# Two blocks of 512 tokens taken together, one inner tile of 1024 tokens at a time

## The chip, the cores and the metric

The kernel runs on one core of a Trainium2 chip. The metric is device time in microseconds, the median over timed runs. Before the change it is 786.54 us (two runs, 785.62 and 787.46). One further execution was taken by the hardware profiler; all durations below come from that one.

The engines of the core are TensorE (PE in the rows: matmuls, with the weight loads shown apart as PEld), VectorE (DVE), ScalarE (ACT), GpSimd (POOL, here mostly the issuer of DMAs) and SyncE (SP, an issuer of DMAs). Each runs its own instructions in program order and waits on semaphores for the others.

## The reference

`x` has 8 batches of 3008 tokens by 256 channels, `filt_r` and `filt_i` 1505 x 256. All in float32:

```python
X = np.fft.rfft(x, axis=1)
y = np.fft.irfft(X * (filt_r + 1j * filt_i)[None], n=3008, axis=1)
h = y.reshape(24064, 256) @ w_in            # w_in 256 x 2048
g = np.maximum(h, 0) + alpha * np.minimum(h, 0)
out = g @ w_out                             # w_out 2048 x 256
```

So there is a filter along the sequence by Fourier transforms, and then a two-layer network with a leaky activation whose slope `alpha` differs from one inner unit to the next.

## The kernel before

**The transforms.** 3008 is 47 x 64, and the transforms are matmuls with constant matrices in float16. Per batch there are 16 pieces A (`piece_a`, one matmul of 512 columns), 12 pieces B (`piece_b`, two matmuls of 256 columns; then two DVE multiplications with the filter, `ww` and `uu`, L232 and L233, which read PSUM; then two accumulating DMAs from POOL that join the complex parts, L235), 12 pieces C (`piece_c`, two matmuls of 256) and 16 pieces D (`piece_d`, four matmuls of 94 columns). Between A and B and between C and D the data goes through DRAM to be turned. D leaves `yT`, the input of the network with channels on partitions; it holds two batches. Pieces A, C and D are copied out of PSUM by ACT. They share two PSUM banks (`psF`), whose order is the string `BANKS`.

**The network.** The tokens are taken in 48 blocks: 512 tokens, and 384 in one of every twelve so that two batches make twelve blocks. A block has 16 steps. In step `j`, `up` multiplies 128 inner units by the block: two matmuls of 512 columns (L497) into one half of a PSUM tile `hps` of two banks; there are two such tiles. After every odd step ACT copies the two inner tiles, 128 x 1024, to float16 in `gtb` (L505). DVE then forms `m = min(g, 0) * (alpha - 1)`, in two instructions of 512 because the two inner tiles have different slopes (L508, slopes in `alm_s`), and adds it, `g += m`, in one instruction of 1024 (L509). In what follows one such copy with its DVE instructions is called a **unit**; a block of 512 tokens has eight. `gtb` holds two blocks; `m` has two buffers.

**The second layer** of a block runs one block later, woven into the steps of the next (`LAG` 16 steps; the loop sends its matmuls until `done` reaches `(step - 16) / 16` blocks). A plain block sends 64 matmuls of 256 columns (`eight`, L534). A block in `FAST` uses seven products of half size in place of eight (`seven`, L556): 112 matmuls of 128 columns, on the quarters `a11, a21, a12, a22` of `g` and on combinations of them and of the weights. The combinations of the weights are computed once (`combine`, into `tw_s`). Those of `g` are four sums, each in two halves `h`: `z1 = a21 + a22` and `z2 = z1 + a11` on DVE (L517, L519), `a21 += a11` and `a12 += z2` by accumulating DMAs from POOL (L521, L523). At the end of a fast block ACT copies partial products out (five copies of 256) and DVE joins them by a subtraction and an addition in float32 (L476). 21 of the 48 blocks are fast, up to block 38 every second one.

**The order** is written out by hand: 48 x 16 = 768 steps, and tables (`STEPS_A` to `STEPS_X`, `FIRST` for the first batches, `SUMS` and `TAIL` for the sums) that say before which step a piece goes. In a step come, in this order, the joining operations left over (`flush`), the sums that are due, the pieces that are due, the two `up` matmuls, and the second layer's matmuls up to `done`. Batch 0 is transformed before step 0 by a method of its own (`First`) while the constants arrive.

Of the kernel before, what the change touches and what calls it, by code (L numbers as in the profile page):

```python
# [13 lines left out]
NFFT = 3008  # L14
# [8 lines left out]
    "010101010101010101010101010101001010010110010010101010101010101010110101101010101010101011010101"  # L23
    "010101010101010101010110110101001011010101011010110111010010101010101010010110100010101110101101"
    "010010101100101010010101010101010101001101010101010010110111010110101010101010101010101010101001"
    "010101010100101101101010010101010101010101010101010101100101101010110100100010100101010101010101"
    "01010101010101101010101101001110101010101010101010101010"
)
STEPS_A = (-84, -81, -77, -76, -65, -59, -58, -58, -56, -53, -52, -51, -50, -48, -46, -43)
STEPS_B = (-21, -15, 4, 6, 13, 21, 25, 27, 32, 40, 54, 55)  # L30
STEPS_C = (2, 10, 16, 19, 24, 33, 35, 46, 62, 63, 70, 70)
STEPS_D = (89, 89, 90, 91, 92, 94, 95, 98, 100, 101, 105, 113, 118, 125, 144, 147)
STEPS_T = (0, 0, 2, 2, 13, 17, 19, 21, 21, 35, 40, 43)
STEPS_E = (6, 6, 7, 11, 23, 27, 29, 29, 53, 54, 55, 56)
STEPS_N = (24, 29, 35, 37)
STEPS_K = (118, 121, 128, 133, 143)
STEPS_X = ((20, 27, 42, 52), (107, 109, 113, 126))
FIRST = (
# [61 lines left out]
def kernel(  # L100
# [90 lines left out]
    def obank():  # L191
        ob[0] ^= 1
        return psO[ob[0]].tile([128, 2, D], FP32, name="op")

    class Fft:
        def __init__(self, b):
            self.b = b
# [529 lines left out]
```

## Time and profile before

| | |
|---|---|
| median of the timed runs | 786.54 us |
| profiled execution, its own time | 781.17 us |
| its span, first to last instruction | 779.1 us |
| granted TensorE clock | 1.000 |
| ACT busy, 902 instructions | 605.1 us (78%) |
| POOL busy, 361 instructions | 273.4 us (35%) |
| DMA moved | 122.93 MB, mean 158 GB/s |

Busy time is the union of an engine's instruction times. Instructions of one engine overlap in the rows: a duration is from start to the end of the last write, while the next may start earlier. What an engine needs is therefore counted by pitches, the distance from one start to the next in a stretch without idle time. "x" counts instructions. A release after an arrow names what ended the idle time before an instruction.

### The profile page before, as it was taken

What the parts mean: (1) busy time and instruction counts of PE and PEld (TensorE: products, weight loads), DVE (VectorE), ACT (ScalarE), POOL (GpSimd) and SP (SyncE); (2) the same over time, 40 slices, a digit from 0 to 9 for tenths busy, and PEclk for the clock granted to TensorE, in tenths of its full rate; (3) what the DMA queues carried; (4) which work ended last, traced back from release to release, by engine and by line L of the source; (5) the groups of instructions that cost most, each with busy time, mean ns of one, the idle gap of its engine ahead of it and who ended that gap; (6) DMA issues with size and microseconds to landing.
All of it is one profiled execution on the core that took longest, in us unless ns stands there. A gap on an engine that the chain in (4) does not pass through costs nothing.

```text
span 779.1 us, 18298 instructions
## 1 busy us (share of the span) xinstructions
PE 759.0 (97%) x6952; PEld 540.7 (69%) x6952; DVE 687.3 (88%) x1501; ACT 605.1 (78%) x902; POOL 273.4 (35%) x361
## 2 busy tenths in 40 slices
PE   7898999999999999999999999999999999999998
PEld 6755667666677767766667767767667777777766
DVE  4786996799999999899899989989899999889994
ACT  4687778888878887788868887788878777787763
POOL 7720542144244341453324423434223434102210
PEclk9999999999999999999999999999999999999999
DMA  9994868766997779975799769886797555735642
GB/s 192 187 224 121 163 121 189 207 123 146 198 211 169 147 152 199 214 164 122 163 215 190 147 136 196 197 169 130 162 204 171 109 116 95 181 86 110 121 96 68
DMA packets 114959, 122.93 MB, mean 158 GB/s; under 512 B 12776, under 2 KB 94456, under 8 KB 114744
## 3 DMA queue, kind: packets, MB, share of 16 engines
q0 software_dynamic: 34736, 52.19, 40.8%
q1 hardware_dynamic: 79992, 69.52, 33.4%
q8 instruction: 54, 0.88, 0.5%
q14 instruction: 33, 0.27, 0.1%
q10 hardware_dynamic: 144, 0.07, 0.0%
HBM read 56.06 MB, written 46.66 MB: 132 GB/s over the span
## 4 chain that ended last, share of the span: by engine, by line
PE 80%; DVE 7%; DMA 7%; ACT 3%; issue 2%; POOL 1%; DVEq 0%; ACTq 0%; POOLq 0%
PE hps L497 36%; PE op L534 20%; PE op L556 14%; PE psF L209 3%; DMA gtb<-ss 3%; PE psF L272 2%; PE psF L247 2%; PE psF L229 2%; DVE m L508 2%; DVE gtb L509 2%; ACT gtb L505 2%; DMA a_dram<-asb 1%; DMA filt_s<-in_filt_r_dram 1%; DVE ww L232 1%; DVE uu L233 1%
## 5 line engine op out<-in xcount | busy, mean ns | idle before, releaser
L505 ACT ACTIVATE gtb<-hps 128x1024 f16<-128x1024 f32 (+1 forms) x384 | 386.3, 1006 | 104.4 <-PE hps L497 101.9
L497 PE MATMUL hps<-yT,win_s 128*128 128x512 f16 (+1 forms) x1536 | 449.2, 374 | 0.0
L508 DVE TENSOR_SCALAR m<-gtb,alm_s 128x512 f16<-128x512 f16 (+1 forms) x768 | 235.6, 349 | 48.5 <-ACT gtb L505 46.5
L509 DVE TENSOR_TENSOR gtb<-gtb,m 128x1024 f16<-128x1024 f16 (+1 forms) x384 | 261.6, 681 | 17.2
L534 PE MATMUL op<-wout_s,gtb 128*128 128x256 f16 x1600 | 243.3, 272 | 0.0
L534 PEld LDWEIGHTS <-gtb 128*128 128x128 f16 x1600 | 156.1, 98 | 105.1
L235 POOL DMA_DIRECT2D uu<-ww x168 | 141.1, 1038 | 246.9 <-DVE uu L233 125.2
L497 PEld LDWEIGHTS <-win_s 128*128 128x128 f16 x1536 | 136.6, 98 | 25.7 <-issue 2.7
L556 PEld LDWEIGHTS <-gtb 128*128 128x128 f16 x1680 | 114.4, 98 | 55.1 <-DMA gtb<-ss 2.5
L521 POOL DMA_DIRECT2D gtb<-gtb x42 | 41.8, 994 | 193.7 <-DVE ss L517 74.3
L556 PE MATMUL op<-wout_s,gtb 128*128 128x128 f16 x1008 | 85.6, 219 | 2.3 <-DMA gtb<-ss 1.7
L279 ACT ACTIVATE asb<-psF 96x512 f16<-96x512 f32 x112 | 65.4, 594 | 14.5 <-PE psF L209 10.8
L279 ACT ACTIVATE yT<-psF 128x376 f16<-128x376 f32 x120 | 57.0, 488 | 11.0 <-PE psF L272 10.3
L556 PEld LDWEIGHTS <-ss 128*128 128x128 f16 x672 | 47.1, 98 | 23.3
L556 PE MATMUL op<-tw_s,gtb 128*128 128x128 f16 x672 | 58.0, 219 | 0.0
L556 PE MATMUL op<-tw_s,ss 128*128 128x128 f16 x672 | 58.0, 219 | 0.0
L232 DVE TENSOR_TENSOR ww<-psF,filts_s 128x512 f16<-128x512 f32 x84 | 57.4, 683 | 0.0
L233 DVE TENSOR_TENSOR uu<-psF,filt_s 128x512 f16<-128x512 f32 x84 | 57.2, 681 | 0.0
L279 ACT ACTIVATE v<-psF 128x512 f16<-128x512 f32 x84 | 49.7, 598 | 8.7 <-PE psF L247 7.9
L167 POOL DMA_DIRECT2D xs<-in_x_dram x64 | 41.4, 969 | 23.6 <-PE psF L209 11.7
L523 POOL DMA_DIRECT2D gtb<-ss x42 | 45.2, 1264 | 4.7 <-PE op L556 2.4
L272 PE MATMUL psF<-wi_s,zt 96*128 96x94 f16 x504 | 39.6, 205 | 4.4 <-ACT asb L279 3.1
(85 smaller groups left out, 517.8 us busy)
## 6 DMA issues: line engine op xcount, KB each, us to landing
out_dram<-osb SPq DMA_DIRECT2D x127, 128.0 KB
xs<-in_x_dram POOLq DMA_DIRECT2D x64, 188.0 KB, 7.5
a_dram<-asb SPq DMA_DIRECT2D x28, 384.0 KB
uu<-ww POOLq DMA_DIRECT2D x168, 64.0 KB, 3.2
v_dram<-v SPq DMA_DIRECT2D x112, 96.0 KB
zt<-v_dram SPq DMA_DIRECT2D x28, 384.0 KB
gtb<-gtb POOLq DMA_DIRECT2D x42, 256.0 KB, 4.0
gtb<-ss POOLq DMA_DIRECT2D x42, 256.0 KB, 5.9
```

The source lines that it names most:

```text
L232: nc.vector.tensor_mul(ww, px, filts_s[:, 2 * kp : 2 * kp + 2])
L233: nc.vector.tensor_mul(uu, px, filt_s[:, 2 * kp : 2 * kp + 2])
L235: nc.gpsimd.dma_start(out=uu[o : o + 64], in_=ww[64 - o : 128 - o], accum_op=OP.add)
L272: nc.tensor.matmul(ps[:, m], self.zt[g][:, 4 * mh + m, dh * 128 : dh * 128 + 128], wi3_s, start=True, stop=True)
L279: nc.scalar.activation(o, i, AF.Copy)
L497: nc.tensor.matmul(self.hps[:, j % 2, 0:tn], win_s[:, kt, j * 128 : (j + 1) * 128], yT[:, kt, self.t0 : self.t0 + tn], start=(kt == 0), st ...
L505: nc.scalar.activation(g, hs, AF.Copy)
L508: nc.vector.tensor_scalar(ms[:, i], g[:, i], 0.0, a, OP.min, OP.mult)
L509: nc.vector.tensor_add(g, g, ms)
L523: nc.gpsimd.dma_start(out=a12, in_=z2, accum_op=OP.add)
L534: nc.tensor.matmul(op[:, si % 2], self.pair(k // 2)[:, k % 2, 128 * si : 128 * si + 128], wout_s[:, k], start=(k == 0), stop=(k == 15))
L556: nc.tensor.matmul(acc[:, 128 * i : 128 * i + 128], x[:, k, 128 * i : 128 * i + 128], b[:, k], start=first and k + i == 0, stop=k == 7, sk ...
```

## The change

From step 128 on, the blocks of 512 tokens are taken in pairs (block 12, of 384, and block 47, of 256, are single). A pair has 32 steps, two for each of the 16 inner tiles. In a step both blocks are multiplied by one half (`kt`) of the inner tile's weights; after the second step the tile `hps` holds one inner tile of 1024 tokens, which has one slope. ACT copies it, DVE forms `m` in one instruction of 1024 and adds in one of 1024 (`up_two`). A unit is still 128 x 1024; the numbers of ACT copies and of `up` columns stay.

- The second layer of a pair's first block starts 32 steps after the pair's first step (`PACE`); up to step 160 it is sent at 1/18 of a block per step.
- 29 blocks are fast, among them all from 26 to 45. The sum `a21 += a11` goes from POOL's DMA to DVE (entries with 5 in the tables), `a12 += z2` in six cases too (`VEC`). The order of the seven products is new, and ACT copies the second partial sum to SBUF, where DVE adds, in place of a DVE addition that reads PSUM.
- `yT` holds one batch. A block that crosses the end of a batch is multiplied in two parts (`parts`): five blocks, 32 more matmuls each.
- `gtb` is six groups of half a block; `m` has one buffer, `osb` four.
- The pieces of batches 3 to 7 go 16 steps earlier, and all tables are new. The input of batch 1 is loaded ahead of `w_out`; the copies that complete `twi_s` and `filts_s`, and a copy of `twf_s` out of `gtb`, go into steps 9 to 28.

```diff
-FAST = frozenset((8, 10, 12, 14, 16, 18, 20, 22, 24, 26, 28, 30, 32, 34, 36, 38, 40, 42, 43, 44, 45))
-SUMS = ((9, 1, 0), (10, 3, 0), (16, 2, 0), (17, 1, 1), (17, 3, 1), (19, 2, 1), (20, 4, 0), (21, 4, 1))
-TAIL = ((12, 1, 0), (12, 3, 0), (18, 1, 1), (18, 3, 1), (18, 2, 0), (18, 2, 1), (20, 4, 0), (21, 4, 1))
-LAG = 16
+FAST = frozenset((13, 14, 17, 18, 19, 21, 22, 23, 24, 26, 27, 28, 29, 30, 31, 32, 33, 34, 35, 36, 37, 38, 39, 40, 41, 42, 43, 44, 45))
+ONE = ((9, 1, 0), (10, 5, 0), (16, 2, 0), (17, 1, 1), (17, 5, 1), (19, 2, 1), (20, 4, 0), (21, 4, 1))
+TWO_A = ((28, 1, 0), (29, 2, 0), (30, 5, 0), (33, 1, 1), (34, 2, 1), (35, 5, 1), (35, 4, 0), (36, 4, 1))
+TWO_B = ((44, 1, 0), (45, 1, 1), (45, 2, 0), (46, 2, 1), (47, 5, 0), (48, 5, 1), (51, 4, 0), (52, 4, 1))
...
+VEC = ((22, 4, 0), (22, 4, 1), (28, 4, 0), (29, 4, 0), (36, 4, 0), (37, 4, 0))
+SHIFT = 16
+XSTEP = -8
+
+
+def PACE(step):
+    return (step - 16) / 18 if step < 160 else (step - 32) / 16
+
+
...
-    p_osb = ctx.enter_context(tc.tile_pool(name="p_osb", bufs=3))
+    p_m = ctx.enter_context(tc.tile_pool(name="p_m", bufs=1))
+    p_osb = ctx.enter_context(tc.tile_pool(name="p_osb", bufs=4))
     psH = ctx.enter_context(tc.tile_pool(name="psH", bufs=2, space=bass.MemoryType.PSUM))
...
-    twf_s = konst.tile([128, NK1, 192], FP16, name="twf_s")
+    twf_s = konst.tile([128, NK1, 128], FP16, name="twf_s")
...
-    gtb = konst.tile([128, 2, 8192], FP16, name="gtb")
+    gtb = konst.tile([128, 6, 4096], FP16, name="gtb")
+    twf_w = gflat[:, 14336 : 14336 + 192 * NK1].rearrange("p (k c) -> p k c", c=192)
...
-    yT = konst.tile([128, 2, 2 * NFFT], FP16, name="yT")
+    yT = konst.tile([128, 2, NFFT], FP16, name="yT")
...
-                nc.tensor.matmul(px[:, kh], twf_s[:, k1, 64:192], self.at[:, k1], start=True, stop=True)
+                nc.tensor.matmul(px[:, kh], twf_s[:, k1], self.at[:, k1], start=True, stop=True)
...
-            t0 = self.base + g * 752
+            t0 = g * 752
...
+    for c in range(4):
+        xc[(1, c)] = load_x(1, c)
     for q in range(2):
         nc.gpsimd.dma_start(
             out=wout_s[:, 8 * q : 8 * q + 8],
             in_=moe_w_out[1024 * q : 1024 * q + 1024].rearrange("(j p) d -> p j d", p=128))
-    for c in range(4):
-        xc[(1, c)] = load_x(1, c)
-    nc.gpsimd.dma_start(out=twi_s[64:128], in_=twx_s[64:128])
-    for o in (0, 64):
-        nc.gpsimd.dma_start(out=filts_s[o : o + 64], in_=filt_s[64:128])
...
-    sizes = [512] * 5 + [384] + [512] * 6
+    sizes = [(512,)] * 5 + [(384,)] + [(512,)] * 2 + [(512, 512)] * 2 + [(384,)] + [(512, 512)] * 17 + [(256,)]
...
+            self.made = 0
+            self.sent, self.total = 0, 112 if self.fast else tn // 8
+            self.gr, self.have = [], set()
+            o = t0 % NFFT
+            cut = min(tn, NFFT - o)
+            self.parts = [(0, cut, o)] + ([(cut, tn, 0)] if cut < tn else [])
+
+        def quad(self, kh):
+            return gtb[:, self.gr[kh]].rearrange("p (l t k c) -> p l t k c", l=2, t=2, k=4)
+
+        def inner(self, l, t, k):
+            return self.quad(k // 4)[:, l, t, k % 4]
...
+        def up(self, acc, j, kt):
...
+            for i, (ca, cb, o) in enumerate(self.parts):
+                nc.tensor.matmul(acc[:, ca:cb], win_s[:, kt, j * 128 : (j + 1) * 128],
+                                 yT[:, kt, o : o + cb - ca], start=(kt == 0 and i == 0), stop=(kt == 1),
+                                 skip_group_check=True)
...
         def sums(self, w, h):
+            (a11, a21), (a12, a22) = [[self.quad(h)[:, l, t] for t in range(2)] for l in range(2)]
             k = slice(4 * h, 4 * h + 4)
...
+            step, dma = w if w < 5 else w - 2, w < 5 and (self.n, w, h) not in VEC
...
+            if step == 1:
                 nc.vector.tensor_add(z1, a21, a22)
-            elif w == 2:
+            elif step == 2:
+                assert (1, h) in self.have
                 nc.vector.tensor_add(z2, z1, a11)
-            elif w == 3:
-                nc.gpsimd.dma_start(out=a21, in_=a11, accum_op=OP.add)
             else:
-                nc.gpsimd.dma_start(out=a12, in_=z2, accum_op=OP.add)
+                a, z = (a21, a11) if step == 3 else (a12, z2)
+                if dma:
+                    nc.gpsimd.dma_start(out=a, in_=z, accum_op=OP.add)
+                else:
+                    nc.vector.tensor_add(a, a, z)
...
-            yield from product(q, a12, b21, True)
-            yield from product(r, a11, b11, True)
-            s1 = p_osb.tile([128, 2, D], FP32, name="osb")
+            yield from product(q, 1, 0, 0, b21, True)
+            yield from product(q2, 1, 1, 0, t4, True)
+            s1, o2 = (p_osb.tile([128, 2, D], FP32, name="osb") for _ in range(2))
+            nc.scalar.activation(o2[:, :, 0:128], halves(q2), AF.Copy, scale=-1.0)
+            yield from product(r, 0, 0, 0, b11, True)
             nc.scalar.activation(s1[:, 0], r, AF.Copy)
-            yield from product(q2, a22, t4, True)
-            o2 = p_osb.tile([128, 2, D], FP32, name="osb")
-            nc.scalar.activation(o2[:, :, 0:128], halves(q2), AF.Copy, scale=-1.0)
-            yield from product(r, ss[:, 1], n2, False)
+            yield from product(q2, 0, 0, 1, n1, True)
+            nc.scalar.activation(o2[:, :, 128:256], halves(q2), AF.Copy, scale=-1.0)
+            yield from product(r, 0, 1, 2, n2, False)
             nc.scalar.activation(s1[:, 1], r, AF.Copy)
+            yield from product(q2, 1, 0, 4, b22, False)
+            o1 = p_osb.tile([128, 2, D], FP32, name="osb")
+            o = o1.rearrange("p i (h c) -> p h i c", h=2)
+            nc.scalar.activation(o, bq.rearrange("p h (i c) -> p h i c", i=2), AF.Copy)
+            late.append((nc.vector.tensor_add, (o, o, s1.rearrange("p h (i c) -> p h i c", i=2))))
+            late.extend((store, (self.t0 + 128 * i, o1, i)) for i in range(2))
+            yield from product(r, 0, 1, 3, t3, False)
...
+    def up_two(pair, step):
+        j, kt = step // 2, step % 2
+        if step % 16 == 0:
+            for blk in pair:
+                blk.gr.append(int(next(groups)))
+        k, l = j // 2, j % 2
+        ga, gb = sorted(blk.gr[k // 4] for blk in pair)
+        if step % 16 == 1:
+            free.remove(ga)
+            free.remove(gb)
+        if kt == 0:
+            pair[0].hps = psH.tile([128, 2, 512], FP32, name="hps")
+        for blk in pair:
+            blk.up(pair[0].hps[:, int(blk.gr[k // 4] == gb)], j, kt)
+        if kt == 1:
+            g = gtb[:, ga : gb + 1 : gb - ga].rearrange("p a (l t k c) -> p a l t k c", l=2, t=2, k=4)[:, :, l, :, k % 4]
+            m = p_m.tile([128, 2, 512], FP16, name="m")
+            hs, ms = (t.rearrange("p a (t c) -> p a t c", t=2) for t in (pair[0].hps, m))
+            nc.scalar.activation(g, hs, AF.Copy)
+            nc.vector.tensor_scalar(ms, g, 0.0, alm_s[:, j : j + 1], OP.min, OP.mult)
+            nc.vector.tensor_add(g, g, ms)
+            for blk in pair:
+                blk.made += 1
...
+    for i in range(2):
+        k = slice(12 * i, 12 * i + 12)
+        put(STEPS_W[i], nc.vector.tensor_copy, twf_s[:, k], twf_w[:, k, 64:192])
...
+    def swapped(ka, kb):
+        for o in (0, 64):
+            nc.gpsimd.dma_start(out=filts_s[o : o + 64, ka:kb], in_=filt_s[64:128, ka:kb])
+
+    put(STEPS_F[0], lambda: nc.gpsimd.dma_start(out=twi_s[64:128], in_=twx_s[64:128]))
     for i in range(4):
+        put(STEPS_F[1 + i], swapped, 6 * i, 6 * i + 6)
...
-        p = 96 * (b - 1)
+        p = 96 * (b - 1) - SHIFT * (b > 2)
...
+    def down(step):
+        while todo and done[0] < PACE(step):
+            blk, it = todo[0]
+            try:
+                done[0] += next(it)
+                if blk.sent == blk.total:
+                    free.update(blk.gr)
+                    blk.sent += 1
+            except StopIteration:
+                todo.pop(0)
...
+    for unit in sizes:
+        blks = []
+        for i, tn in enumerate(unit):
+            blk = Block(n, t0, tn, len(unit) == 1 and n not in FAST)
+            if blk.fast:
+                table = (ONE, TWO_A, TWO_B)[len(unit) - 1 + i]
+                for st, w, h in table:
+                    ahead.setdefault(at + st, []).append((blk, w, h))
+            blks.append(blk)
+            n, t0 = n + 1, t0 + tn
...
+        for step in range(at, at + 16 * len(unit)):
+            sums(step)
             for fn, args in plan.pop(step, ()):
                 fn(*args)
+            if len(unit) == 1:
+                up_one(blk, step - at)
+            else:
+                up_two(blks, step - at)
+            down(step)
+        at += 16 * len(unit)
+        todo.extend((blk, blk.items()) for blk in blks)
+    last, _ = todo.pop()
+    while todo:
+        sums(at)
+        down(at)
+        at += 1
     flush()
-    blk.finish()
-    assert not plan
+    last.finish()
+    assert not plan and not ahead
```

More of the change, by code (lines that the diff above doesn't have):

```diff
@@ L668 @@
         put(STEPS_K[n], combine, n)
[L669 to L681 removed]
+    todo, ahead = [], {}
@@ new lines, with sums @@
+    done = [0.0]
+    def sums(step):
+        flush()
+        for b, w, h in ahead.pop(step, ()):
+            b.sums(w, h)
+    def down(step):
[8 more added lines that the diff above has]
+                todo.pop(0)
+    n, t0, at = 0, 0, 0
+    for unit in sizes:
[10 more added lines that the diff above has]
+            sums(step)
```

191 lines of the change are left out of this document (79 added, 112 removed), and 24 rows, old and new, of the table FIRST.

## The prediction, made before the changed kernel was run

> **What bounds the kernel now.** I first read the granted clock (1.000 throughout, so pitches can be compared across the run), then the page's busy times and chain:
>
> ```profile
> PE 759.0 (97%) x6952; PEld 540.7 (69%) x6952; DVE 687.3 (88%) x1501; ACT 605.1 (78%) x902; POOL 273.4 (35%) x361
> ...
> PE 80%; DVE 7%; DMA 7%; ACT 3%; issue 2%; POOL 1%; DVEq 0%; ACTq 0%; POOLq 0%
> ```
>
> TensorE is the bound, with VectorE next. Whether PE really streams is seen from pitches in its timeline (start, duration, line, form, count):
>
> ```profile
> 306.74 0.60 PE L534 MATMUL op<-wout_s,gtb 128*128 128x256 f16 x4
> 307.18 0.59 PE L497 MATMUL hps<-yT,win_s 128*128 128x512 f16 x2
> 307.61 0.60 PE L534 MATMUL op<-wout_s,gtb 128*128 128x256 f16 x4
> ...
> 752.01 0.59 PE L497 MATMUL hps<-yT,win_s 128*128 128x512 f16 x2
> 752.44 0.55 PE L556 MATMUL op<-tw_s,gtb 128*128 128x128 f16 x7
> 752.83 0.59 PE L497 MATMUL hps<-yT,win_s 128*128 128x512 f16 x2
> ```
>
> Start to start, two matmuls of 512 take 0.434 us, four of 256 also 0.434, seven of 128 take 0.388: 217, 108.5 and 55.4 ns each, proportional to columns. So weight loads are hidden, and a fast block's second layer costs 112 x 0.0554 = 6.20 us against 64 x 0.1085 = 6.95 for a plain one: 0.74 us per fast block.
>
> Next I cut the run into three stages. ACT's copies L505 count the steps (one per two): the 193rd and the 369th start at 416.9 and 740.7 us, which are steps 384 and 736. Busy us by stage, in the order span, PE, PEld, DVE, ACT, POOL:
>
> ```profile
> 38.40:416.90 378.50, 369.84 (x3160) 256.80 (x3159) 335.50 (x739) 305.54 (x455) 136.23 (x176) 1.00 0.80 171
> 416.90:740.70 323.80, 322.90 (x3063) 230.07 (x3061) 301.08 (x669) 257.80 (x383) 104.19 (x124) 1.00 0.70 147
> 740.70:779.10 38.40, 34.94 (x332) 25.79 (x329) 27.80 (x64) 20.45 (x25) 3.49 (x4) 1.00 0.37 83
> ```
>
> In the middle stage PE has 0.9 us to spare in 323.8, DVE 22.7. The question is whether the change asks DVE for more than that. DVE's pitches come from its timeline:
>
> ```profile
> 177.17 0.42 DVE L663 TENSOR_SCALAR tw_s<-tw_s 128x1024 f16<-128x1024 f16 x1
> 177.50 0.61 DVE L508 TENSOR_SCALAR m<-gtb,alm_s 128x512 f16<-128x512 f16 x2
> ...
> 721.05 0.61 DVE L508 TENSOR_SCALAR m<-gtb,alm_s 128x512 f16<-128x512 f16 x2
> 721.69 0.69 DVE L509 TENSOR_TENSOR gtb<-gtb,m 128x1024 f16<-128x1024 f16 x1
> 722.30 0.61 DVE L508 TENSOR_SCALAR m<-gtb,alm_s 128x512 f16<-128x512 f16 x2
> ```
>
> and the width of one instruction from its groups kept apart by form (count, busy us, mean ns, idle before):
>
> ```profile
> L508 DVE TENSOR_SCALAR m<-gtb,alm_s 128x512 f16<-128x512 f16 x704 | 218.0, 352 | 40.8 <-ACT gtb L505 39.1
> L508 DVE TENSOR_SCALAR m<-gtb,alm_s 128x384 f16<-128x384 f16 x64 | 17.6, 317 | 7.7 <-ACT gtb L505 7.3
> ```
>
> A unit is 0.64 (the pair L508 to L509) + 0.61 (L509 to the next) = 1.25 us. Inside the pair the second starts after 0.26 (0.61 less its own 0.35), and L509, which waits for it, 0.38 later: a dependent start costs 0.12 more. Sums, joins and the filter's `ww` and `uu` go at 0.60 each, so a piece B is 1.2. Check on the middle stage: 176 units x 1.25 = 220.0; 34 pieces B x 1.2 = 40.8; by the tables 49 sums and 19 joins x 0.6 = 40.8; in all 301.6, where the row has 301.08. The same count for PE (352 steps of 0.434 for `up`, the second layer, the pieces) gives 322.0 where the row has 322.90. The method holds, and a stage lasts as long as its fuller engine.
>
> **The change, part by part.**
>
> *The wide tile.* Two L508 become one of 1024. Its time: 128 more columns cost 35 ns (317 to 352), so 512 more cost 0.14, and TS-to-add becomes 0.38 + 0.14 = 0.52; the unit is 0.52 + 0.61 = 1.13 against 1.25. From below there is L663, 1024 wide with constants and nothing dependent on it: 0.33, a unit of 0.94. From above, two instructions as now: 1.25. I take 1.125, since slope and dependent start are both rows of the same instruction.
>
> *One buffer for `m`.* The next TENSOR_SCALAR overwrites what the add before it still reads. Either the order on the engine is enough and it costs nothing, or it starts like a dependent instruction, 0.11 later (0.69 of the add plus 0.03, against 0.61). By the tables 75 of the middle stage's 176 units follow the last one with nothing between: 0 to 8.2 us. I take half, 4, for want of a row that shows it.
> [...]
>
> *29 fast blocks and the sums on DVE.* A fast block now brings six sums to DVE where it brought four, two joins as before, and six more from `VEC`. In the middle stage of the new tables: 176 x 1.125 = 198.0; 31 pieces B = 37.2; 132 sums = 79.2; 42 joins (21 fast blocks) = 25.2. Together **339.6 us**. PE: `up` 152.8, 21 fast and one plain second layer 137.1, pieces 30.4: 320.3. ACT, by the same count 262. So VectorE becomes the bound there, and the stage goes from 323.8 to 339.6: **+15.8**. Its slack before (22.7) was larger than its load saved (22 on units, 4 on pieces B) less its load added (64). DVE can lag behind PE for some steps, since the second layer reads `g` 32 steps later, but each piece B ties them together: PE cannot reuse that `psF` bank before `uu` has read it. What lag is saved up is a few us.
>
> *First stage.* By step 384 the new pace has sent 22 blocks, 6 of them fast, where the old one sent 23, 8 fast (-6.95 + 1.5), and the pieces, earlier by 16 steps, add 2.5: PE -3.0. In steps 224 to 255 DVE needs 31.2 against PE's 28.6: +2.6. Together -0.4. The loads and copies moved into steps 9 to 28 go past POOL's filter DMAs and x loads; the one large stall there now is PE's 3.1 us behind an `asb` save. I leave it as it is and give the start 3 us either way.
>
> *Split blocks.* 64 extra matmuls in the first stage. Matmuls of 94 columns run at 41.5 ns, 2 more than their columns, so 0.2 to, at a whole weight load of 98 ns each, 6 us; I take 0.3. The other 96 lie where PE has 19 us to spare.
>
> *ACT and POOL.* ACT gains one copy of 512 (0.6) per fast block: hidden, 77 us of room in the middle stage. POOL loses 42 DMAs of `a21` and gains 10 of `a12`: off the path.
>
> *Last stage.* Steps 736 on: 22.9, one plain second layer and its rest 7.4, the 256-token end 32 x 0.1085 = 3.5, in all 33.8; before 27.1 + 7.0. -0.3.
>
> **The sum.** -0.4 + 0.3 + 15.8 + 4 - 0.3 = +19.4, taken as +19. The span becomes 798, the profiled execution's own time 781.2 + 19 = 800.2. The median of the timed runs lies 5.4 above that execution; kept, it gives **805.5 us**, 2.4% slower. Differences under 2% (15.7 us) are not told from no change here. With the unit between 1.06 and 1.125 and `m` between 0 and 8, the forecast alone spans 790 to 810.
>
> **The rivals.**
>
> 1. *PE stays the bound (not slower).* If the wide instruction goes at L663's pitch, the unit is 0.94, DVE needs 307 in the middle stage, and PE's 320.3 decides: -3.5 there, and the 2.6 of the first stage goes: -6.5 in all, **780**. It decides below a unit of 1.015. For it: L663 is as wide and as many partitions. Against it: L508 reads its slope from SBUF and is waited for. Chance 0.16.
> [...]
>
> 2. *PE starves as well.* `a12 += z2` is issued 8 steps ahead of its product (10 before) and lands in 5.9 us at the median, 8.7 at most, after 1.2 of issue; behind a DVE that lags, POOL issues it late, and `uu`'s DMAs queue behind it. One us more for half of the 29 blocks, on top: **820**. For it: the rows already have PE waits on it of up to 1.2. Against: PE has 19 us of room. Chance 0.14.
>
> 3. *The wide form is slow.* Its input is now four runs of 256 with two strides. At half the rate per column, 0.27 more per unit, 176 times: 47 more, **850**. Today's fast blocks read two runs of 256 at 347 ns, like plain ones. Chance 0.05.
>
> The forecast has 0.60; 0.05 is for the start or something unseen. **Range 788 to 820**: it leaves out half of rival 1, rival 3 and part of rival 2. Slower by over 2%: two thirds of the forecast, rivals 2 and 3: 0.60. Within 2%: the rest of it and rival 1: 0.37. Faster: 0.03, as even rival 1 gains 0.8%.
>
> **What would show it.** In the changed profile: one TENSOR_SCALAR of 128x1024, near 0.49 us, its add 0.52 after it; DVE at 95% or more between steps 384 and 736, PE idle there and released by DVE or by what DVE feeds; that stage near 340 us; the next TENSOR_SCALAR 0.61 (no wait) or 0.72 after an add. The prediction is wrong if that unit is near 1.0, or if DVE idles in that stage.

## The result: 838.4 us, 6.6% slower, and the profile after

The changed kernel takes 838.40 us (two runs, 838.40 and 838.41), the kernel before 786.54 beside it: a ratio of 1.066, 95% interval 1.061 to 1.071. The forecast was 805.5 with a range of 788 to 820. The direction was right, the size was not: 52 us came where 19 were forecast.

The profiled execution of the changed kernel lies close to its runs: 838.4 us, its span 836.5. That of the kernel before was 5.4 faster than its median, so the spans differ by 57.4, and it is these 57.4 that the stages below add up to. The page's first line, busy us, share of the span and count of each engine:

```profile
PE 770.0 (92%) x7496; PEld 552.3 (66%) x7496; DVE 722.7 (86%) x1311; ACT 624.8 (75%) x954; POOL 248.9 (30%) x335
```

No engine is as full as TensorE was before (97%). The busy time of each engine in the three stages of the prediction, cut at steps 0, 384, 736 and the end (span, PE, PEld, DVE, ACT, POOL, then the granted clock):

```profile
39.60:428.50 388.90, 372.32 (x3105) 255.73 (x3104) 330.46 (x632) 309.98 (x461) 125.38 (x165) 1.00 0.72 156
428.50:795.70 367.20, 332.48 (x3591) 240.13 (x3589) 341.07 (x588) 274.87 (x422) 88.73 (x106) 0.98 0.56 117
795.70:836.50 40.80, 33.95 (x396) 28.78 (x393) 27.69 (x61) 18.16 (x30) 3.43 (x4) 0.95 0.37 85
```

The middle stage has 367 us, and in it neither TensorE (332) nor VectorE (341) is busy throughout. Busy time leaves out what passes between two instructions of which the second waits for the first (in the rows from 301.25 us on, shown below, 0.03 us from the end of a TENSOR_SCALAR to its add and 0.11 from there to the next TENSOR_SCALAR). By its list of waits (us in total, times, longest) VectorE stands idle for only 9.5 us of the 367:

```profile
DVE m L662 <- ACT gtb L661: 8.5, 7, 5.9
DVE gtb L663 <- PE hps L515: 0.5, 1, 0.5
DVE gtb L663 <- DVE m L662: 0.5, 1, 0.5
```

So VectorE sets the pace, TensorE waits for it, and now and then VectorE waits in its turn.

TensorE's own work can be counted: every matmul in the trace by its columns, at the pitches of a stretch without idle time (0.2165 us for 512, 0.1085 for 256, 0.0555 for 128, 0.0415 for 94). What a stage lasts beyond that is lost to waiting, or to a lower clock. Before, the exact steps 384 and 736 are at 418.5 and 742.3 us; the prediction's cuts lay one unit earlier.

| stage | work before | length before | work after | length after | lost before | lost after |
|---|---|---|---|---|---|---|
| steps 0 to 256 | 247.1 | 259.0 | 239.4 | 254.3 | 11.9 | 14.9 |
| steps 256 to 384 | 118.1 | 121.2 | 122.3 | 134.7 | 3.1 | 12.4 |
| steps 384 to 736 | 321.2 | 323.7 | 319.2 | 367.2 | 2.5 | 48.0 |
| steps 736 to the end | 32.9 | 36.8 | 32.1 | 40.8 | 3.9 | 8.7 |

So the change does save TensorE work, 6.2 us over the run (719.2 to 713.0), and loses ten times that: 62.6 us more of waiting and of lower clock. Step 0 comes 1.3 later. -6.2 + 62.6 + 1.3 = 57.7, against 57.4 in the spans.

What TensorE waited for, from the list of its waits (us in total, times, longest):

```profile
PE op L576 <- DVE gtb L663: 18.7, 13, 3.6
PE psF L261 <- DVE uu L247: 7.7, 5, 4.0
PE psF L261 <- DMA uu<-ww: 7.6, 4, 3.9
PE psF L243 <- DVE uu L247: 4.8, 5, 1.3
PE psF L286 <- DVE uu L247: 3.2, 5, 1.0
```

L576 is the seven products, L663 the add that completes `g`; L261, L243 and L286 are pieces C, B and D, L247 is `uu`. The list has two stories. The first is the products of a pair's second layer waiting for the pair's last inner tiles. In the timeline (start, duration, engine, line, form, count; in brackets the idle time before and its release) at step 691:

```profile
751.40 0.69 DVE L663 TENSOR_TENSOR gtb<-gtb,m 128x1024 f16<-128x1024 f16 x1
752.13 0.69 DVE L533 TENSOR_TENSOR ss<-gtb 128x1024 f16<-128x1024 f16 x1
752.15 0.29 PE L576 MATMUL op<-wout_s,gtb 128*128 128x128 f16 x2 [2.42 <-DVE gtb L663]
```

The add ends at 752.09 and the matmul starts 0.06 later: it waited for exactly this unit. Such gaps stand at the start of every pair near the end, at steps 563, 595, 627, 659, 691, 722 and 754, of 2.2, 1.4, 1.0, 1.1, 2.4, 3.5 and 3.6 us. The second story is piece C, at steps 342, 434 to 438, 531 to 534 and 627. The wait at step 438:

```profile
479.30 0.68 DVE L247 TENSOR_TENSOR uu<-psF,filt_s 128x512 f16<-128x512 f32 x1
...
480.27 1.70 POOL L249 DMA_DIRECT2D uu<-ww  x2 [4.63 <-DVE uu L247]
...
487.96 0.58 PE L261 MATMUL psF<-uu,twi_s 128*128 128x256 f16 x2 [3.86 <-DMA uu<-ww]
...
488.34 1.06 PE L515 MATMUL hps<-yT,win_s 128*128 128x512 f16 x2
...
492.20 0.48 DVE L662 TENSOR_SCALAR m<-gtb,alm_s 128x1024 f16<-128x1024 f16 x1 [5.90 <-ACT gtb L661]
```

A batch's last piece B now stands at step 62 of its table and the last piece C at 70; before, 55 and 70. VectorE lags (the piece's matmuls start at 474.90, `uu` at 479.30), POOL can only then issue the DMAs that join the parts, and they land while the load of the next turned data goes on. TensorE stands for 3.86 us, and, since nothing new reaches ACT in that time, VectorE then stands for 5.90: the engine that was too full idles because the engine that feeds it has stopped. VectorE's lag is only one part of this delay. With some 35 us of VectorE's work left out (e13 below) the waits for this DMA at steps 342, 438 and 534 are 2.9, 4.3 and 2.2 us, where here they are 2.4, 3.9 and 0.9.

The largest wait at a piece C, at step 627, has another release:

```profile
679.42 0.38 PE L243 MATMUL psF<-at,twf_s 128*128 128x256 f16 x2
...
687.74 0.68 DVE L247 TENSOR_TENSOR uu<-psF,filt_s 128x512 f16<-128x512 f32 x1
...
688.47 0.38 PE L261 MATMUL psF<-uu,twi_s 128*128 128x256 f16 x2 [4.03 <-DVE uu L247]
```

The last piece B is multiplied at 679.42, VectorE comes to it 8 us later, and piece C starts 0.05 after the end of `uu` (688.42). The DMAs of `uu` land 3.0 us after their issue at the median, so piece C does not wait for this `uu` as its input; it waits for the bank of `psF` that VectorE has only then read. In e13 this wait is 2.1 us.

### The profile page after: what moved, and what is told of

Same layout as the page of the kernel before. It is cut to its first block, busy times and chain, and to the rows that moved or that the text cites. A ratio compares the mean times of both kernels' runs of the same rounds, so it can differ in the third digit from the quotient of the medians.

```text
span 836.5 us, 19583 instructions
## 1 busy us (share of the span) xinstructions
PE 770.0 (92%) x7496; PEld 552.3 (66%) x7496; DVE 722.7 (86%) x1311; ACT 624.8 (75%) x954; POOL 248.9 (30%) x335
## 5 line engine op out<-in xcount | busy, mean ns | idle before, releaser
L515 PE MATMUL hps<-yT,win_s 128*128 128x512 f16 (+5 forms) x1696 | 456.0, 359 | 0.1
L661 ACT ACTIVATE gtb<-hps 128x1024 f16<-128x1024 f32 x304 | 311.6, 1025 | 93.0 <-PE hps L515 90.1
L663 DVE TENSOR_TENSOR gtb<-gtb,m 128x1024 f16<-128x1024 f16 x304 | 210.5, 692 | 17.2 <-DVE m L662 0.9
L576 PEld LDWEIGHTS <-gtb 128*128 128x128 f16 x2320 | 159.9, 99 | 90.1 <-DVE gtb L663 23.8
L662 DVE TENSOR_SCALAR m<-gtb,alm_s 128x1024 f16<-128x1024 f16 x304 | 147.9, 486 | 46.9 <-ACT gtb L661 37.4
L553 PE MATMUL op<-wout_s,gtb 128*128 128x256 f16 x1120 | 170.4, 273 | 0.6 <-DVE gtb L663 0.6
L576 PE MATMUL op<-wout_s,gtb 128*128 128x128 f16 x1392 | 123.8, 221 | 19.3 <-DVE gtb L663 18.7
L637 ACT ACTIVATE gtb<-hps 128x1024 f16<-128x1024 f32 (+2 forms) x80 | 75.0, 938 | 24.0 <-PE hps L515 22.8
L576 PEld LDWEIGHTS <-ss 128*128 128x128 f16 x928 | 65.5, 98 | 30.0 <-issue 0.6
L576 PE MATMUL op<-tw_s,gtb 128*128 128x128 f16 x928 | 82.4, 223 | 0.0
L576 PE MATMUL op<-tw_s,ss 128*128 128x128 f16 x928 | 80.7, 220 | 0.0
L639 DVE TENSOR_SCALAR m<-gtb,alm_s 128x512 f16<-128x512 f16 (+2 forms) x160 | 47.4, 338 | 16.0 <-ACT gtb L637 14.0
L247 DVE TENSOR_TENSOR uu<-psF,filt_s 128x512 f16<-128x512 f32 x84 | 57.2, 681 | 0.0
L640 DVE TENSOR_TENSOR gtb<-gtb,m 128x1024 f16<-128x1024 f16 (+2 forms) x80 | 51.1, 639 | 3.2
```

Of the source, the lines that this page charges most:

```text
L247: nc.vector.tensor_mul(uu, px, filt_s[:, 2 * kp : 2 * kp + 2])
L515: nc.tensor.matmul(acc[:, ca:cb], win_s[:, kt, j * 128 : (j + 1) * 128], yT[:, kt, o : o + cb - ca], start=(kt == 0 and i == 0), stop=(kt ...
L553: nc.tensor.matmul(op[:, si % 2], self.weights(k, si), wout_s[:, k], start=(k == 0), stop=(k == 15))
L576: nc.tensor.matmul(acc[:, 128 * i : 128 * i + 128], x[:, 128 * i : 128 * i + 128], b[:, k], start=first and k + i == 0, stop=k == 7, skip_ ...
L637: nc.scalar.activation(g, hs, AF.Copy)
L640: nc.vector.tensor_add(g, g, ms)
```

## The experiments

Times are medians; the kernel before, run beside each set, lay between 784.88 and 787.59. The two theories throughout: VectorE's *load* sets the end (the forecast, only larger), or a *latency* does (the order of the work around the pairs' ends and piece C, the single buffer of `m`, DMAs).

### The single buffer of m

A second buffer of `m` needs room. It was made in two ways. The first takes a buffer from `ww`, with a control that takes the buffer and leaves `m` alone (e1, then e2 with `m` on top):

```diff
-            ww = p_uw.tile([128, 2, D], FP16, name="ww")
+            ww = p_uw.tile([128, 2, D], FP16, name="ww", bufs=2)
```

```diff
-    p_m = ctx.enter_context(tc.tile_pool(name="p_m", bufs=1))
+    p_m = ctx.enter_context(tc.tile_pool(name="p_m", bufs=2))
```

> Control: the changed kernel with two buffers for ww instead of three (this frees the SBUF that a second buffer for m needs), nothing else. Theory (VectorE is the bound from step 384 on, and the one buffer of m makes each TENSOR_SCALAR that directly follows an add start 0.80 us after it instead of 0.61): no effect of ww, 838 +- 4 us. Rival (the loop uu on VectorE, its accumulating DMA, piece C on TensorE is what is slow, whatever VectorE's load): fewer ww buffers make it slower still, 845 or more.

> The changed kernel with two buffers for m (and two for ww). Theory: the add to TENSOR_SCALAR pitch goes from 0.80 back to 0.61 and the unit to 1.13; the middle stage (steps 384 to 736) falls from 367 to 340-348 us, the whole run to 806-816 us; VectorE is still the bound there. Rival 1 (only the load of 29 fast blocks and of the sums counts, the wait on m is hidden in VectorE's idle time): 832-838. Rival 2 (the loop through the DMA): 838, with the same PE waits on uu<-ww.

Measured: 851.08 (ratio to before 1.082, 1.075 to 1.088) and 838.50 (1.065, 1.061 to 1.069). The `ww` buffer was itself worth 12.7 us, most of it ahead of step 256, so only the difference of the two tells: the second `m` buffer is worth 12.6 us. Without the control it would have looked like nothing. Both expectations missed: e1 came out where the rival had put it, though 10.8 of its loss lie ahead of step 256, and in e2 the middle stage fell to 358.4, not to 340 to 348.

The second way takes the room from the copies of partial products: `s1` gets one float16 tile of its own, and `osb` three buffers in place of four (e5).

```diff
-    p_m = ctx.enter_context(tc.tile_pool(name="p_m", bufs=1))
-    p_osb = ctx.enter_context(tc.tile_pool(name="p_osb", bufs=4))
+    p_m = ctx.enter_context(tc.tile_pool(name="p_m", bufs=2))
+    p_osb = ctx.enter_context(tc.tile_pool(name="p_osb", bufs=3))
+    p_s1 = ctx.enter_context(tc.tile_pool(name="p_s1", bufs=1))
...
+            s1 = p_s1.tile([128, 2, D], FP16, name="s1")
```

> The changed kernel with two buffers for m, and three buffers of ww as it had. The room comes from elsewhere: the first partial sums s1 get a tile of their own in float16 (one buffer) and osb three buffers. Theory (one buffer of m costs 0.19 to 0.27 us of VectorE per unit that directly follows another): between the two runs with two ww buffers this was worth 12.6 us, so 838 becomes 822-829, with the add to TENSOR_SCALAR pitch back at 0.61. Rival (the gain there was of another cause): 835 or more.

Measured: 827.91 (1.056, 1.053 to 1.060), 10.5 below the changed kernel. The smaller `osb` and the new `s1` were not run alone; the gain is near the 12.6 of the first way. What the buffer does is seen in VectorE's timeline. With one buffer, in the changed kernel:

```profile
301.25 0.49 DVE L662 TENSOR_SCALAR m<-gtb,alm_s 128x1024 f16<-128x1024 f16 x1
301.77 0.69 DVE L663 TENSOR_TENSOR gtb<-gtb,m 128x1024 f16<-128x1024 f16 x1
302.57 0.49 DVE L662 TENSOR_SCALAR m<-gtb,alm_s 128x1024 f16<-128x1024 f16 x1
303.16 0.69 DVE L663 TENSOR_TENSOR gtb<-gtb,m 128x1024 f16<-128x1024 f16 x1
303.96 0.49 DVE L662 TENSOR_SCALAR m<-gtb,alm_s 128x1024 f16<-128x1024 f16 x1
```

and with two, in e5:

```profile
303.29 0.48 DVE L664 TENSOR_SCALAR m<-gtb,alm_s 128x1024 f16<-128x1024 f16 x1
303.80 0.69 DVE L665 TENSOR_TENSOR gtb<-gtb,m 128x1024 f16<-128x1024 f16 x1
304.41 0.48 DVE L664 TENSOR_SCALAR m<-gtb,alm_s 128x1024 f16<-128x1024 f16 x1
```

From an add to the next TENSOR_SCALAR it is 0.80 us with one buffer (302.57 - 301.77) and 0.61 with two. In the middle stage 69 units follow directly on the last, and 62 of them start 0.80 after its add: 62 x 0.19 = 12 us of VectorE's time.

The same buffer taken from the kernel before (e11):

```diff
-    p_m = ctx.enter_context(tc.tile_pool(name="p_m", bufs=2))
+    p_m = ctx.enter_context(tc.tile_pool(name="p_m", bufs=1))
```

> The kernel before with one buffer for m, nothing else: the price of that buffer where VectorE has room. By the pitches 0.19 to 0.27 us for each unit that directly follows another, in the middle stage 76 of 176: 14 to 20 us of its 22 us of idle time. If the idle time covers it, 785-792; if it meets the fast blocks, where VectorE is full, 793-803.

Measured: 791.61 (1.009, 1.006 to 1.013). There 93 units of the middle stage follow directly, and 69 of them start 0.80 after the add: at most 69 x 0.19 = 13 us of VectorE's time, and the stage grows by 6. The price is the same; what it is worth is less where VectorE has room.

### VectorE's load

`a21 += a11` back on POOL's DMAs, first alone (e3), then with two buffers of `m` and two of `ww` (e4):

```diff
-            step, dma = w if w < 5 else w - 2, w < 5 and (self.n, w, h) not in VEC
+            step, dma = w if w < 5 else w - 2, (self.n, w, h) not in VEC
```

> The changed kernel with the sum a21 += a11 back on an accumulating DMA of POOL, one buffer of m kept. Takes 44 x 0.6 = 26 us of VectorE work out of the middle stage, leaves the wait on m, which then comes more often since fewer instructions lie between units. Theory: the middle stage 338-348 us, the run 803-818. Rival 1 (load alone): VectorE's need falls below PE's 320, so the run comes to 785-795. Rival 2: 838 or more, as 58 more DMAs queue on POOL.

> Both: two buffers of m (two of ww), and a21 += a11 by DMA. Theory: VectorE needs 339.6 - 26 = 313 us in the middle stage, less than PE's 320; PE is the bound again, the stage 322-330 us, the run 780-795 us, no better than the kernel before by more than 1%. Rival 2 (the loop through the DMA): still above 815.

Measured: 827.42 (1.051, 1.046 to 1.057) and 837.95 (1.063, 1.058 to 1.068). Alone it takes 11.0 us off, of 58 x 0.6 = 35 that leave VectorE, less than the theory and its first rival had expected. The list of waits of e3 says where the rest went:

```profile
PE psF L261 <- DMA uu<-ww: 17.1, 7, 4.5
PE op L576 <- DMA gtb<-ss: 10.4, 12, 2.2
PE op L576 <- DVE gtb L663: 4.8, 7, 1.9
```

The wait for the add falls from 18.7 to 4.8, and in its place TensorE waits for DMAs that share POOL's queue with the new ones: for `uu`'s (17.1 in place of 7.6) and for `gtb<-ss` (10.4, where the changed kernel has 0.6). `gtb<-ss` is `a12 += z2`, which was on POOL before; it now lands 6.2 us after its issue at the median, in place of 4.3. For `a21 += a11` itself (`gtb<-gtb`) no product waits. e4 came out where the DMA rival had put it, above 815. If the `ww` buffer costs 12.7 here too, e4 against e3 leaves 2.2 for `m`: where VectorE is less often the later one, the second `m` buffer is worth little.

To take the load away with nothing in its place, the sum `a21 += a11` was left out (e13):

```diff
-                else:
+                elif w != 5:
                     nc.vector.tensor_add(a, a, z)
```

> The kernel after with the sum a21 += a11 left out altogether (the second layer of the fast blocks is then not the reference's; TensorE's work is the same, and no DMA takes the sum's place). If VectorE's load is what the long stage waits for, 42 sums x 0.6 = 25 us go between steps 384 and 736 and some 16 x 0.6 ahead of step 384, of which 4 to 6 come back because more units then follow one another directly and pay 0.19 for the single buffer of m: 808 to 816, the middle stage 343 to 349. If the order of the work (products that read the last inner tiles of a pair, pieces C close behind B) or the DMAs decide, less than 10 us go: 828 or more.

To add a load alone, the wide instruction was taken as two of 512 (e14):

```diff
-            nc.vector.tensor_scalar(ms, g, 0.0, alm_s[:, j : j + 1], OP.min, OP.mult)
+            for i in range(2):
+                nc.vector.tensor_scalar(ms[:, i], g[:, i], 0.0, alm_s[:, j : j + 1], OP.min, OP.mult)
```

> The kernel after with VectorE's TENSOR_SCALAR of 1024 taken as two of 512 again, as in the kernel before (same slope twice). If VectorE's load decides, 0.12 us per unit come on top: 176 x 0.12 = 21 between steps 384 and 736, and up to 8 ahead of it, 858 to 868. If something else decides, less than 10 come: below 848.

Measured: 816.90 (1.040, 1.035 to 1.046), 21.5 less than the changed kernel; and 867.34 (1.105, 1.099 to 1.110), 28.9 more. 58 sums of 0.6 are 34.8 us, and 304 units of 0.12 are 36.5: of the load taken away 62% comes back as time, of the load added 79%. (Without the sums more units follow one another directly and pay 0.19 for the buffer: 106 start 0.80 after an add in the whole run, 100 in the changed kernel.) The middle stage of e13 and of e14 (same columns as above):

```profile
426.80:777.00 350.20, 331.12 (x3589) 240.24 (x3587) 317.20 (x546) 273.86 (x422) 88.14 (x106) 0.98 0.58 123
```

```profile
434.50:820.20 385.70, 335.85 (x3590) 242.40 (x3588) 365.50 (x765) 275.34 (x422) 88.49 (x106) 0.96 0.53 111
```

VectorE's load is the main thing: 828 and 848 were the points at which the latency theory would have begun, and both runs lie on the other side. In e14 VectorE's waits sum to 3.3 us of the stage's 385.7: with more load the stage is VectorE's need and little else. Load isn't alone, though. e13 gains slightly less than load alone had forecast (816.9 where 808 to 816 was expected), and its middle stage still lasts 350 with 319.2 us of TensorE work and 317 of VectorE's busy time: the waits for `uu`'s DMA, 10.3 us, are now the largest.

```profile
PE psF L261 <- DMA uu<-ww: 10.3, 4, 4.3
PE op L576 <- DVE gtb L663: 7.5, 7, 2.1
```

What the wide instruction is worth without the rest, in the kernel before (e15; one slope for two inner tiles):

```diff
-                for i in range(2):
-                    a = alm_s[:, j - 1 + i : j + i]
-                    nc.vector.tensor_scalar(ms[:, i], g[:, i], 0.0, a, OP.min, OP.mult)
+                nc.vector.tensor_scalar(ms, g, 0.0, alm_s[:, j : j + 1], OP.min, OP.mult)
```

> The kernel before with one TENSOR_SCALAR of 1024 in place of two of 512 (one slope for both inner tiles, so the activation is not the reference's; nothing else changes). If TensorE bounds the kernel before, the VectorE time saved (0.12 x 352 = 42 us) buys nothing: 783 to 787. If VectorE's latency costs there too, 780 or less.

Measured: 783.88 (0.997, 0.995 to 1.000). In the middle stage

```profile
422.50:745.50 323.00, 322.75 (x3061) 229.87 (x3059) 281.74 (x493) 257.45 (x381) 107.75 (x125) 1.00 0.70 146
```

VectorE's 301 became 282, and the stage went from 323.7 to 323.0: TensorE is the bound of the kernel before, and what VectorE saves there buys nothing.

### The order around piece C

The last piece B of a batch from step 62 to 56 (59 for batch 4), 14 steps ahead of the last piece C (e6), and the same with e5 (e7):

```diff
-            put(p + steps_b[kp], f.piece_b, kp)
+            put(p + (steps_b[kp] if kp < 11 or b < 4 else 59 if b == 4 else 56), f.piece_b, kp)
```

> The changed kernel with the last piece B of batches 4 to 7 moved from step 62 to 56 of the batch (59 for batch 4), that is 14 steps ahead of its piece C at 70 where the change has 8 (15 before); one buffer of m kept. Theory B (that piece's accumulating DMAs are caught by the load of the next batch's turned data, so PE waits for them at piece C, VectorE runs dry behind it and PE's clock falls): the waits of PE at piece C near steps 342, 438, 530 and 626 vanish (14 us of direct waits) and the run falls to 820-828. Theory A alone (VectorE is simply full, waits only move): the time lost at piece C comes back at the next pair's start, 833-838.

> Both edits: two buffers of m (three of ww) and the last piece B at step 56. If the two causes add: 804-814. VectorE then needs 339.6 us in the middle stage by the count of the prediction, so that stage should come near 340-346. If they cover the same time: 820-825.

Measured: 832.44 (1.061, 1.059 to 1.064), 6.0 less than the changed kernel; 819.17 (1.044, 1.041 to 1.048), 19.2 less. The two repairs add up, and a little more (10.5 + 6.0 = 16.5), but both expectations were missed: e6 lies between the two theories, and e7, with a middle stage of 352, above the 804 to 814 of two causes that add. From the list of waits of e6:

```profile
PE op L576 <- DVE gtb L663: 23.7, 14, 3.9
PE psF L261 <- DMA uu<-ww: 5.5, 6, 1.6
...
PE psF L261 <- DVE uu L247: 0.8, 2, 0.6
```

At piece C the wait for VectorE falls from 7.7 to 0.8 and the one for `uu`'s DMA from 7.6 to 5.5, its longest from 3.9 to 1.6. The wait of L576 for the add rises from 18.7 to 23.7, which would fit a lag that is no longer paid at C and is then due at the pair's end.

Then `a21` by DMA on top of both (e10):

> Both edits, all 29 fast blocks, and a21 += a11 by DMA: VectorE needs 313 us in the middle stage, PE 320. If VectorE's load alone decides, PE is the bound and the run comes to 788-798. If taking the sums from VectorE only moves the wait to POOL's DMAs, as the runs with one of the edits suggest (827 and 838 with two ww buffers), 808-820 with PE waits on gtb<-ss.

Measured: 811.04 (1.033, 1.029 to 1.037), 8.1 below e7. The list of waits:

```profile
PE op L577 <- DMA gtb<-ss: 17.1, 17, 2.2
PE op L577 <- DVE gtb L665: 2.7, 4, 1.1
```

In e7 the wait for the add is 16.6. It falls to 2.7, and 17.1 of waits for `gtb<-ss` stand in its place, again for `a12 += z2` and not for the sum that was moved. They stand 12 and 13 steps into a fast block's second layer, at the sixth of its seven products, and the DMA lands 6.2 us after its issue at the median. Neither place tried for `a21 += a11` is free with 29 fast blocks: VectorE is full, and on POOL's queue it delays `a12 += z2`.

### The fast blocks

With both repairs, every second block fast from 28 on, 20 in all (e8); and only the first block of each pair, 17 in all (e9):

```diff
-FAST = frozenset((13, 14, 17, 18, 19, 21, 22, 23, 24, 26, 27, 28, 29, 30, 31, 32, 33, 34, 35, 36, 37, 38, 39, 40, 41, 42, 43, 44, 45))
+FAST = frozenset((13, 14, 17, 18, 19, 21, 22, 23, 24, 26, 27, 29, 31, 33, 35, 37, 39, 41, 43, 45))
```

```diff
+FAST = frozenset((13, 15, 17, 19, 21, 23, 25, 27, 29, 31, 33, 35, 37, 39, 41, 43, 45))
```

> Both edits, and from block 28 to 44 only every second block fast (20 fast blocks in all). Takes 9 x 8 instructions of 0.6 us = 43 us off VectorE and adds 9 x 0.74 = 6.7 us to PE. Theory A (VectorE's load is the bound from step 384 on): PE becomes the bound there, its 320 plus 7 = 327 us, the run 784-796. Theory B alone (stalls by placement of pieces): no gain over the run with both edits, 804-814 plus up to 7.

> The changed kernel with both edits (two buffers of m, the last piece B at step 56) and only the first block of every pair from 13 to 45 fast: 17 fast blocks. Against the run with 20 fast blocks it takes 5 x 8 x 0.6 = 24 us off VectorE between steps 256 and 448 and adds 3 x 0.74 = 2.2 us to PE in all. Theory (VectorE's load is what costs, wherever fast blocks stand in a row): steps 256 to 512 fall from 259 us to 248-252, the run from 799 to 788-793. Rival (those stages are slow by where the pieces stand): 799-803.

Measured: 799.04 (1.019, 1.015 to 1.023) and 796.10 (1.014, 1.010 to 1.018). Nine fast blocks fewer give TensorE 6.6 us more to do, and the kernel becomes 20.1 us faster. Both runs lie between the theory and its rival: VectorE's load is most of it, and not all. In e9 the middle stage is

```profile
427.70:758.00 330.30, 328.39 (x3109) 236.68 (x3108) 290.65 (x505) 263.12 (x382) 76.24 (x90) 1.00 0.54 117
```

TensorE streams again (328.39 of 330.30), VectorE is busy for 40 us less than the stage lasts: the picture of the kernel before, at 4 fast blocks fewer. Last, the six blocks from 40 on all fast with `a21` by DMA (e12):

```diff
+FAST = frozenset((13, 15, 17, 19, 21, 23, 25, 27, 29, 31, 33, 35, 37, 39, 40, 41, 42, 43, 44, 45))
...
+            step, dma = w if w < 5 else w - 2, (w < 5 or self.n >= 40) and (self.n, w, h) not in VEC
```

> As the run with 17 fast blocks, but all blocks from 40 to 45 fast, with their a21 += a11 by DMA: 20 fast blocks. From step 640 on no piece B loads VectorE; it needs about 24 us per pair there against PE's 26.7. Expect 2 us less than with 17 fast blocks: 785-791; at best level with the kernel before.

Measured: 797.33 (1.015, 1.011 to 1.019): no gain over e9, where 785 to 791 was expected. None of the versions is faster than the kernel before.

### How the 52 us divide, and what is open

One after the other: the second `m` buffer and the last piece B together 19.2 (838.4 to 819.2); nine fast blocks out of the row from 28 on 20.1 (to 799.0); three more between 13 and 27, 2.9 (to 796.1). That leaves 10.6 to the kernel before, 785.55 beside e9. The stages of e9 say where these lie, in the profiled executions, whose spans differ by 16.4 (795.5 against the 779.1 of the kernel before): 2.5 us are TensorE work (721.7 against 719.2, four fast blocks fewer), 6 are lost ahead of step 128 (135.9 us, 119.0 of them work, where before loses 10.7), 4 between steps 256 and 384, and 4 in the start and the other stages together. What sets the loss ahead of step 128 is open: of the kernels with three buffers of `ww`, whose code is much the same up to there, that stage lasts between 131.7 and 135.9, and no run was made for it.

## Why the prediction was right in direction and wrong in size

**The bound before, right.** e15 bears it out: 19 us off VectorE's busy time in the middle stage bought 0.7.

**The wide tile, right.** The group of the changed kernel (count, busy us, mean ns, idle before):

```profile
L663 DVE TENSOR_TENSOR gtb<-gtb,m 128x1024 f16<-128x1024 f16 x304 | 210.5, 692 | 17.2 <-DVE m L662 0.9
...
L662 DVE TENSOR_SCALAR m<-gtb,alm_s 128x1024 f16<-128x1024 f16 x304 | 147.9, 486 | 46.9 <-ACT gtb L661 37.4
```

486 ns where 0.49 was forecast, and the add 0.520 us behind it at the median, where 0.52 was. A few are later, so that 176 of them take 95.6 us in place of 91.5: 4 us that were not foreseen and whose cause is open. Rival 1 needed a unit below 1.015 and rival 3 one of 1.4; with two buffers of `m` it is 1.13.

**One buffer of `m`, under-sized, and the bound itself was wrong.** The prediction's upper end was 0.11 per unit, by the rows of L508 to L509, where a dependent instruction starts 0.03 after the end of the one before. Here the TENSOR_SCALAR starts 0.11 after the end of the add: 0.19 per unit, 12 us where at most 8.2 had been allowed and 4 taken. One row of another pair of instructions was taken as a ceiling, and it isn't one.

**VectorE as the new bound, right; "a stage lasts as long as its fuller engine", wrong.** This is the step that failed. VectorE's need was forecast at 339.6. Add the 12 us of the `m` buffer and the 4 of late adds, and it is 356; TensorE's need was 320.3, by the count 319.2. The stage took 367.2: the remaining 11 are nearly all VectorE's own waits, 9.5 us, 5.9 of it in one, behind the stall at piece C. So of the 23.6 by which the stage misses its forecast (323.8 + 15.8 + 4 = 343.6), some 12 are need that was counted too low (8 for the buffer, 4 for late adds) and some 11 are this step. The maximum of two engines is a floor, reached only when the fuller one never waits. Here it waits because the engine that feeds it has been stopped, in part by its own lag.

**"The second layer reads `g` 32 steps later", wrong.** This was the reason to let VectorE lag without a price. It holds for a pair's first inner tiles. The first products of the second layer take the last ones too, so VectorE's lag has to be repaid every 32 steps, at the pair's end: 18.7 us in 13 waits. The last stage's forecast (-0.3, measured +4.0) failed at the same place, with 3.6 us at step 754.

**"Each piece B ties them together", right, and priced too low.** The waits for a bank that `uu` has not yet read are there: in the list above 7.7 us at C, 4.8 at B and 3.2 at D, the largest 4.03 at step 627. They were to bound the lag at a few us; it grew to 8. What the prediction didn't look at is the other half, the 7.6 us that piece C waits for `uu`'s DMA: the new tables put the last B 8 steps ahead of the last C.

**The first stage, wrong.** Forecast -0.4, measured +8.8 (254.3 + 134.7 against 259.0 + 121.2). Up to step 256 it gains 4.7. Between 256 and 384 it loses 13.5: 4.2 are TensorE work that now lies there, the rest the same waits as later (piece C at step 342 alone 2.4). The second `m` buffer and the earlier piece B bring that part from 134.7 to 128.5 in e7. The prediction looked for VectorE's overload in steps 224 to 255, ahead of this part, found 2.6 there, and took nothing for the steps up to 384.

**Split blocks, right.** 448 columns and 64 take 0.190 + 0.0285 us where 512 take 0.2165: 0.002 each.

**ACT and POOL, off the path, right in the main.** ACT had 274.87 us in the middle stage where 262 was counted. The sums moved to and from POOL cost one wait of 0.6; `uu`'s DMAs, which POOL issues, are the 7.6 above.

**Rival 2, the wrong transfer.** It was near in time (820) and not in its mechanism: the products waited 0.6 us once for `a12`. The late transfer was `uu`'s. Waits for `a12` of 2 us and more in all come only in e3 (10.4), e4 (11.5), e10 (17.1) and e12 (2.0), where `a21` shares the queue.

**The sum.** 19.4 forecast; 8 more for `m`, 4 for late adds, 11 for VectorE's waits in the middle, 9 in the first stage, 4 in the last, 1 at the start: 56.4 of the 57.4 by which the spans differ. Of its signs, TensorE does wait for VectorE and what it feeds; but VectorE is busy for 93% of the stage and not 95%, the stage lasts 367 and not 340, and the next TENSOR_SCALAR comes 0.80 after an add and not 0.61 or 0.72.

## What to carry to other kernels

When work moves from a full engine to one with some room, the sum of that engine's needs gives only a floor: look for the points where the first one must wait for the last result of the second (here the end of each pair, and the last piece B ahead of the last piece C), for there the lag is due, and the engine that was behind can then starve in its turn (here VectorE, for 5.90 us). Leave some room on the second: with VectorE's need at 94% of TensorE's work (before, 301 of 321) TensorE streamed, at 112% (356 of 319) the stage was 48 us longer than TensorE's work, and not 37. And price a buffer that is taken away by a run with it alone, on the kernel before.

## What the runs showed of the hardware

**A wait on the same engine.** A TENSOR_SCALAR behind an add of 128x1024 starts 0.61 us after the add's start when its target is free, 0.80 when it must wait until that add has read it; the add itself lasts 0.69. In the kernel before, with one buffer (e11), the same 0.80 appears with two instructions of 512.

**The clock after a stall.** Behind TensorE's gap of 3.86 us in the changed kernel its matmuls of 512 go at half speed: two of them and the four of 256 behind them take 0.85 us each (488.34 to 489.19), not 0.434, for about 3.4 us: from 491.56 on two of 512 take 0.44 again (491.56 to 492.00). In windows of 4 us (the clock is the third number from the end):

```profile
484.00:488.00 4.00, 0.14 (x2) 0.07 (x2) 2.05 (x4) 0.72 (x1) 0.00 (x0) 0.99 1.01 243
488.00:492.00 4.00, 4.00 (x17) 2.10 (x18) 0.00 (x0) 1.46 (x2) 0.00 (x0) 0.58 0.54 133
492.00:496.00 4.00, 4.00 (x30) 2.83 (x29) 3.73 (x7) 2.55 (x4) 0.86 (x2) 1.00 0.54 155
```

A shorter gap may do it too, and later: behind 2.23 us at 619.7 the first matmuls are at full speed, from 621 on they are slow, up to 624.4, and no other gap of over 1 us is near.

```profile
619.70 0.28 PE L576 MATMUL op<-wout_s,gtb 128*128 128x128 f16 x2 [2.23 <-DVE gtb L663]
...
620.27 0.60 PE L515 MATMUL hps<-yT,win_s 128*128 128x384 f16 x3
...
621.86 1.06 PE L515 MATMUL hps<-yT,win_s 128*128 128x384 f16 x3
```

Behind 2.39 us at 384.47 the granted clock is 0.51 from 386 to 389. Behind the 2.42 us at 752.15 nothing slows. Over the whole run the granted clock is 0.985 (before 1.000), at most 0.015 x 836.5 = 12.5 us of TensorE's time; how much of it VectorE used to catch up was not measured.

**The same DMA, at the median and beside a load.** Over the whole run the DMAs of `uu` land 3.0 us after their issue at the median. The pair of them issued at 480.27 let TensorE go on at 487.96, 7.7 us later. The mean busy share of the DMA engines from 470 to 500 us, in 40 slices (9 is 90% or more), and the load issued at 475.3 in the same answer:

```profile
DMA  6689400639999999999999932428830299999999
...
at<-a_dram SPq DMA_DIRECT2D x4, 384.0 KB
```

From 477 to 487 us the share is 90% or more, and the DMA lands within 1 us of the end of that stretch. That the load of 4 x 384 KB is the cause was not tried by a run of its own.
